# Attention in pairs of query tiles over four quarters of the array, with a softmax split over three engines and due times derived backwards

## Chip, cores, metric

One core of a Trainium2 chip. The metric is the device time of one launch in microseconds (us). The kernel before takes 608.16 us (median of 3 runs, 606.42 to 609.38). Five engines run their own queues in order: TensorE (PE; PEld is its weight load), VectorE (DVE), ScalarE (ACT), GpSimd (POOL) and SyncE (SP, which here issues the DMAs).

## What is computed

A windowed attention with block summaries, then two dense stages. The input has 2 batches, 8 heads, 768 positions and 64 dimensions, all fp32:

```python
k_sum = k.reshape(B, H, nb, 32, D).max(axis=3)
v_sum = v.reshape(B, H, nb, 32, D).mean(axis=3)
scores_l = where(|i - j| < 16, scale * q @ k.T, -1e9)
scores_s = scale * q @ k_sum.T + log(32)
a = softmax(concat([scores_l, scores_s]))
x = (a @ concat([v, v_sum])) as (1536, 512)
x = ((x @ w1) * (x @ w2)) @ w3 @ w_out      # widths 1024, 1024, 512
h = x @ w_in;  y = (h * clip(h + 3, 0, 6) / 6) @ w_out2
```

## The kernel before

Dense products run as three passes of fp32r matmuls: each operand is split into a high and a low part (`arena[:, s, 0]` and `[:, s, 1]`), and high x high, low x high and high x low are added. A weight chunk arrives as raw 64-bit data (512 KB into one of 4 `raw` buffers) and `convert` makes the two parts: ACT (L248, L254), DVE (L263, L267), ACT again (L271, high part), POOL (L275, low part). While the array has banks to spare (the W' part), the first steps of `convert` work in PSUM banks 4 and 5; later they work in the SBUF buffers `c`.

The parts of the program, in order of their data:

- **W'.** `wprime` multiplies w3 with w_out (transposed chunks, group 0 then group 1, 8 steps each, 12 matmuls a step, 24 chunks converted in all); `wprime_out` writes each group's 4 result banks as weights.
- **Attention.** `attend` works on one tile of 64 queries of all 8 heads. Per tile: `scores` (L405, 8 matmuls, one head in the upper 64 rows and columns of the array, the next in the lower, into bank 6), mask and maximum on DVE (L413, L418), 4 exponentials on ACT that also sum (L424), the inverse on DVE (L432, L433), the scaling on POOL (L438), 4 transposes on PE (L446, bank 7), a copy on ACT (L451), 8 matmuls with the values (L458, bank 7), and the split of the result into x's high part on ACT (L470) and low part on DVE (L474). 24 tiles; 8 make one block of 512 tokens. For the first block, keys are copied out of `kres` by DVE (L379); the summaries come from maxima on DVE (L310) and a chain of halving adds on POOL (L323).
- **First dense stage.** `ab(j, i)` multiplies block j of x with chunk i of w1 and w2 (24 matmuls into banks 4 and 5); `acc1` multiplies the product with W' into banks 0 to 3. `x2_out` writes the next x. Block 0's `ab` needs all 8 tiles of block 0 and the first converted w1 and w2 chunks. The tiles of later blocks are laid between the dense matmuls of the block before.
- **Second dense stage.** `hu`, `acc2` and `y_out`, 192 matmuls each of `hu` and `acc2` a block. With W' (192), `ab` (192 a block) and `acc1` (96 a block) that makes 2208 matmuls of 128 x 512 in all.

The order on each engine is not written by hand. Every operation is entered in a graph with its engine, an assumed duration and a **due time**; `Graph.schedule` simulates the engines and always starts the ready operation with the earliest due time. Before, due times come from a handful of constants (`DUE_W`, `DUE_Q`, `AHEAD`, `BEHIND` and others). A DVE or POOL operation marked `lock` waits in that simulation for the SBUF port that the two share.

Of the kernel before, what the change touches and what calls it, by code (L numbers as in the profile page):

```python
# [30 lines left out]
P = 128  # L31
# [9 lines left out]
NK = NWIN + NSUM  # L41
NPAIR = H // 2
# [4 lines left out]
TPK = TB // QT  # L47
# [10 lines left out]
class Graph:  # L58
# [6 lines left out]
    LAT = {"sp": 2100, "pe": 250}  # L65

# [21 lines left out]
    def schedule(self):  # L88
# [55 lines left out]
DUE_W = ((1.47, 2.38), (49.46, 3.51))  # L144
DUE_K, DUE_V, DUE_ROWS = 13.5, 5.9, 14.6
DUE_Q = (28.52, 6.4)
L3N = 1
DUE_FF = 90.7
AHEAD, BEHIND = 461.8, 280.8


def build(tc, qd, kw, vw, kt, vt, consts, wp_in, w12_in, w2_in, out):
# [13 lines left out]
    three = pool.tile([P, 32], F32, name="three")[:, 0:1]  # L166
# [47 lines left out]
    def load(due, out_fn, in_ap, nbytes, writes):  # L214
        g.op("sp", max(650, nbytes / 360.0), due, lambda: nc.sync.dma_start(out=out_fn(), in_=in_ap), (), writes)
# [98 lines left out]
    def sum32(due, x, c, key):  # L314
# [40 lines left out]
    def vsum_rows(due, b, bk):  # L355
        def fn():
            for p in range(NPAIR):
                nc.tensor.transpose(bank[bk][0:NK, p * P : (p + 1) * P], vsum[:, p, :], ident)

        g.op("pe", 460, due, fn, ["vsum", "con"], [("bank", bk)])  # L360

    def summary_cols(due, i, bk):
        g.op(
            "pool", 350, due, lambda: nc.gpsimd.tensor_copy(kall[i][:, :, NWIN:NK], ksum), ["ksum"], [("ks", i)]
        )
        g.op(
            "act", 600, due,
            lambda: nc.scalar.activation(
                out=vall[i][NWIN:NK, :], in_=bank[bk][NWIN:NK, :], func=AF.Copy, scale=1.0 / BLK
            ), [("bank", bk)], [("vs", i)],  # L370
        )

    def copy(eng, n, due, o, i, reads, writes):
        if eng == "act":
            g.op(eng, 190 + 0.86 * n, due, lambda: nc.scalar.activation(out=o, in_=i, func=AF.Copy), reads, writes)
        elif eng == "pool":
            g.op(eng, 60 + 3.5 * n, due, lambda: nc.gpsimd.tensor_copy(o, i), reads, writes)
        else:
            g.op(eng, 200 + 0.52 * n, due, lambda: nc.vector.tensor_copy(o, i), reads, writes, True)  # L379

    def attend(t, due, bs, bp, bx):

        i, i2 = t % 3, t % 2
        tt = t % TPB
        m = 0 if tt == 0 else 2 if tt == TPB - 1 else 1
        j, col = t // TPK, (t % TPK) * QT
        s0 = A_X + NPAIR * j
        ki, vi, si, pi, sti = kall[i], vall[i], sc[i2], pt[i2], st[i2]
        qs = qst[t // 2 % 2]
        if t % 2 == 0:  # L390
            load(due - 5 * us, lambda: qs, qd[t // 2], P * 2048, [("qs", t // 2 % 2)])
        if t < TPK:
            copy("dve", 410, due - 2 * us, ki[:, :, 0:NWIN], kres[:, :, t * QT : t * QT + NWIN],
                 [("kres", c) for c in range(3) if c * S // 3 + (WIN if c else 0) < t * QT + NWIN and t * QT < (c + 1) * S // 3 + WIN],
                 [("kw", i)])
        else:
            load(due - 5 * us, lambda: ki[:, :, 0:NWIN], kw[t], P * NWIN * 16, [("kw", i)])
        load(due - 4 * us, lambda: vi[0:NWIN, :], vw[t], NWIN * 2048, [("vw", i)])
# [11 lines left out]
        g.op("pe", 900, due, scores, [("kw", i), ("ks", i), ("qs", t // 2 % 2)], [("bank", bs)])  # L410

        def mask():
            nc.vector.scalar_tensor_tensor(  # L413
                out=si, in0=bank[bs][:, 0 : NPAIR * NK].rearrange("p (a n) -> p a n", a=NPAIR), scalar=SCALE,
                in1=con[:, m * NK : (m + 1) * NK].unsqueeze(1).to_broadcast((P, NPAIR, NK)),
                op0=ALU.mult, op1=ALU.add,
            )
            nc.vector.tensor_reduce(out=sti[:, 1, :], in_=si, op=ALU.max, axis=AX.X, negate=True)  # L418

        g.op("dve", 1340, due + 1 * us, mask, [("bank", bs), "con"], [("s", i2), ("st", i2)])  # L420

        def expo():
            for p in range(NPAIR):
                nc.scalar.activation(  # L424
                    out=si[:, p, :], in_=si[:, p, :], func=AF.Exp, bias=sti[:, 1, p : p + 1],
                    accum_out=sti[:, 2, p : p + 1],
                )

        g.op("act", 2300, due + 2.5 * us, expo, [], [("s", i2), ("st", i2)])

        def inv():
            nc.vector.tensor_scalar(out=sti[:, 0, :], in0=sti[:, 2, :], scalar1=1e-9, scalar2=None, op0=ALU.add)  # L432
            nc.vector.reciprocal(out=sti[:, 1, :], in_=sti[:, 0, :])  # L433
# [8 lines left out]
        g.op("pool", 1050, due + 4.2 * us, norm, [("st", i2)], [("s", i2)])

        def trans():
            for p in range(NPAIR):
                nc.tensor.transpose(bank[bp][0:NK, p * P : (p + 1) * P], si[:, p, :], ident)  # L446

# [336 lines left out]
```

## Time and profile before

| quantity | before |
|---|---|
| median of 3 runs | 608.16 us |
| profiled execution, own time | 606.42 us |
| its span | 604.6 us |
| PE busy | 573.9 us (95%) |
| DVE, ACT, POOL busy | 287.5, 294.3, 147.1 us |
| PE busy by tenths, first 8 slices of 15.1 us | 3 7 6 7 9 9 6 9, then 9 to the end |

A slice is a fortieth of the span. Busy time counts an instruction from its start to its modelled end, so a busy PE may still be slow; what matters is which engine the others wait for. An execution's own time is its span and a remainder, here 1.82 us.

### The profile page before, as it was taken

To read this page: it belongs to the slowest core of one execution; us is meant where nothing else is said; L and a number is where in the kernel's file an instruction comes from. 1 tells how busy PE (TensorE), PEld (TensorE's weight loads), DVE (VectorE), ACT (ScalarE), POOL (GpSimd) and SP (SyncE) were. 2 spreads that over 40 slices of the span, in tenths; PEclk is the share of its full clock that TensorE was granted. 3 is DMA by queue.
4 is the path that set the end of the run, shared out by engine and by line. 5 is a ranking of instruction groups with operands and counts; after the bars stand their busy time and mean duration, and the time that the engine had idled before them with its cause. 6 is when DMAs were issued, how large, how long until landed. Compare 5 with 4: busy or idle time off the path is not lost.

```text
span 604.6 us, 8171 instructions
## 1 busy us (share of the span) xinstructions
PE 573.9 (95%) x3080; PEld 460.6 (76%) x3080; DVE 287.5 (48%) x443; ACT 294.3 (49%) x645; POOL 147.1 (24%) x144
## 2 busy tenths in 40 slices
PE   3767996999999999999999999999999999999997
PEld 2556774777877777888888888888888888888886
DVE  4587759685774641837455862222222222222221
ACT  6868778774774645617555932222322222322222
POOL 4873434567431113303323430000000000000000
PEclk9897999999999999999999999999999999999999
DMA  8995557565665110532433200000100000100001
GB/s 291 329 292 194 161 169 213 166 203 169 233 214 144 41 28 1 161 118 69 142 140 124 86 0 1 0 1 0 70 1 1 0 1 0 71 0 1 0 1 69
DMA packets 29607, 59.04 MB, mean 98 GB/s; under 512 B 10624, under 2 KB 14080, under 8 KB 29568
## 3 DMA queue, kind: packets, MB, share of 16 engines
q1 hardware_dynamic: 29424, 58.39, 30.1%
q8 instruction: 24, 0.39, 0.3%
q14 instruction: 15, 0.12, 0.1%
q10 hardware_dynamic: 144, 0.13, 0.1%
HBM read 55.37 MB, written 3.15 MB: 97 GB/s over the span
## 4 chain that ended last, share of the span: by engine, by line
PE 89%; DMA 4%; DVE 3%; ACT 2%; issue 1%; POOL 0%; SPq 0%; DVEq 0%; POOLq 0%; ACTq 0%
PE bank L293 81%; DMA raw<-in_wp_dram 4%; PE bank L405 3%; PE bank L458 2%; PE bank L446 2%; ACT raw L254 1%; ACT bank L248 1%; DVE arena L608 1%; DVE c L267 1%; DVE sc L413 0%; DVE c L263 0%; DVE bank L263 0%; ACT arena L271 0%; DVE st L418 0%; DVE ksum L310 0%
## 5 line engine op out<-in xcount | busy, mean ns | idle before, releaser
L293 PE MATMUL bank<-arena 128*128 128x512 f32 x1344 | 334.2, 401 | 18.5 <-ACT arena L271 12.6
L293 PEld LDWEIGHTS bank<-arena 128*128 128x128 f32 x1344 | 253.1, 192 | 77.2 <-ACT arena L271 13.7
L543 ACT ACTIVATE ta<-bank,three 128x512 f32<-128x512 f32 x48 | 33.0, 688 | 149.3 <-PE bank L293 149.3
L293 PE MATMUL bank<-arena,w 128*128 128x512 f32 x432 | 105.4, 396 | 0.0
L547 DVE SCALAR_TENSOR_TENSOR tg<-ta,bank 128x512 f32<-128x512 f32 x48 | 33.0, 688 | 149.3 <-ACT ta L543 149.3
L293 PEld LDWEIGHTS bank<-arena,w 128*128 128x128 f32 x432 | 81.0, 188 | 19.0 <-issue 0.3
L275 POOL TENSOR_TENSOR arena<-c,arena 128x512 fp32r<-128x512 f32 (+1 forms) x50 | 65.2, 1311 | 76.2 <-ACT arena L271 71.4
L492 DVE TENSOR_TENSOR arena<-tg,arena 128x512 fp32r<-128x512 f32 x68 | 55.4, 815 | 37.1 <-ACT arena L487 36.7
L487 ACT ACTIVATE arena<-tg 128x512 fp32r<-128x512 f32 x72 | 45.4, 630 | 37.8 <-DVE tg L547 32.6
L254 ACT ACTIVATE raw<-raw 128x512 uint32<-128x512 uint32 (+1 forms) x74 | 47.7, 653 | 0.0
L438 POOL TENSOR_TENSOR sc<-sc,st 128x480 f32<-128x480 f32 x24 | 24.8, 1031 | 88.8 <-DVE st L433 66.5
L263 DVE SCALAR_TENSOR_TENSOR c<-c,raw 128x512 uint32<-128x512 uint32 x48 | 41.4, 870 | 10.2 <-ACT raw L254 10.0
L267 DVE SCALAR_TENSOR_TENSOR c<-raw,c 128x512 uint32<-128x512 uint32 x48 | 43.9, 931 | 0.5
L511 DVE TENSOR_TENSOR tg<-ta,bank 128x512 f32<-128x512 f32 x24 | 16.5, 687 | 52.8 <-PE bank L293 45.9
L424 ACT ACTIVATE sc<-sc,st 128x120 f32<-128x120 f32 x96 | 36.7, 386 | 8.3 <-DVE st L418 7.2
L248 ACT ACTIVATE c<-raw 128x512 f32<-128x512 f32 x48 | 31.3, 666 | 14.6 <-POOL w L275 5.2
L293 PE MATMUL bank<-w,arena 128*128 128x512 f32 x144 | 35.4, 394 | 0.0
L293 PE MATMUL bank<-late,arena 128*128 128x512 f32 x144 | 34.6, 389 | 0.0
L293 PE MATMUL bank<-arena,late 128*128 128x512 f32 x144 | 34.4, 389 | 0.0
L509 ACT ACTIVATE ta<-bank 128x512 f32<-128x512 f32 x24 | 14.3, 596 | 38.2 <-PE bank L293 38.2
L271 ACT ACTIVATE arena<-c 128x512 fp32r<-128x512 f32 (+1 forms) x50 | 29.9, 607 | 6.0 <-DVE c L267 4.2
L293 PEld LDWEIGHTS bank<-w,arena 128*128 128x128 f32 x144 | 27.0, 188 | 6.4
(48 smaller groups left out, 419.7 us busy)
## 6 DMA issues: line engine op xcount, KB each, us to landing
raw<-in_w_dram SPq DMA_DIRECT2D x48, 512.0 KB, 3.9
raw<-in_wp_dram SPq DMA_DIRECT2D x22, 512.0 KB, 5.5
vall<-in_vw_dram SPq DMA_DIRECT2D x24, 192.0 KB, 2.6
qst<-in_q_dram SPq DMA_DIRECT2D x12, 256.0 KB, 2.8
kall<-in_kw_dram SPq DMA_DIRECT2D x16, 192.0 KB, 3.2
out_dram<-c SPq DMA_DIRECT2D x11, 256.0 KB, 2.0
vres<-in_vt_dram SPq DMA_DIRECT2D x3, 512.0 KB, 6.6
raw<-in_kt_dram SPq DMA_DIRECT2D x3, 512.0 KB, 4.4
```

The costliest lines, as they stand in the source:

```text
L248: lambda uf=uf, wf=wf: nc.scalar.activation(out=uf, in_=wf[:, :, 1], func=AF.Copy, scale=2.0**-112),
L254: lambda lw=lw: nc.scalar.activation(out=lw, in_=lw, func=AF.Copy, scale=2.0**-29 * (1 - eps), bias=7.5 * eps - 0.5),
L263: lambda ui=ui, lw=lw: nc.vector.scalar_tensor_tensor(out=ui, in0=ui, scalar=3, in1=lw, op0=ALU.logical_shift_left, op1=ALU.bitwise_or),
L267: lambda ci=ci, ui=ui, hw=hw: nc.vector.scalar_tensor_tensor(out=ci, in0=hw, scalar=0x80000000, in1=ui, op0=ALU.bitwise_and, op1=ALU.bitwi ...
L271: lambda cf=cf, e=e: nc.scalar.activation(out=slot(s)[:, 0, e], in_=cf, func=AF.Copy),
L275: lambda cf=cf, e=e, eng=eng: eng.tensor_tensor(out=slot(s)[:, 1, e], in0=cf, in1=slot(s)[:, 0, e].bitcast(F32), op=ALU.subtract),
L293: nc.tensor.matmul(out=out_ap, lhsT=lhs(a), rhs=rhs(c), start=start and n == 0, stop=stop and n == 3 * len(terms) - 1,)
L424: nc.scalar.activation(out=si[:, p, :], in_=si[:, p, :], func=AF.Exp, bias=sti[:, 1, p : p + 1], accum_out=sti[:, 2, p : p + 1],)
L487: g.op("act", 630, due, lambda: nc.scalar.activation(out=slot(s)[:, 0, :], in_=src_ap, func=AF.Copy), [src_key], [("t", s, 0)])
L492: lambda: eng.tensor_tensor(out=slot(s)[:, 1, :], in0=src_ap, in1=slot(s)[:, 0, :].bitcast(F32), op=ALU.subtract), [src_key, ("t", s, 0)], ...
L543: g.op("act", 600, due, lambda: nc.scalar.activation(out=t, in_=bank[b], func=AF.Relu, bias=three), [("bank", b), "three"], [("ta", n % 2)])
L547: lambda: nc.vector.scalar_tensor_tensor(out=u, in0=t, scalar=6.0, in1=bank[b], op0=ALU.min, op1=ALU.mult), [("bank", b), ("ta", n % 2)], ...
```

## The change

- Attention works on **pairs** of tiles (12 pairs). `probabilities(u)` holds all up to the probabilities, `attend(u)` the rest. The scores of a pair are 16 matmuls, in groups of four that lie in four different 64 x 64 quarters of the array; the even tile's go to one bank and the odd tile's to another (banks 6 and 7). The keys of a pair are one stretch of 160 with the summaries on both sides, so the even tile has its summaries first and the odd tile last.
- The softmax of a pair is: two masks (DVE, L428), one maximum over 960 columns (DVE, L442), a subtraction (POOL, L444), one exponential (ACT, L445), one sum and the inverse (DVE, L448 to L450), a multiplication (POOL, L454). The transposed probabilities are copied by ACT for the even tile and by DVE for the odd one (L471, L469). The split of x is 512 columns wide.
- Summary rows of the values come from 8 plain matmuls instead of 4 transposes, at two partition offsets.
- **Due times.** Only PE's operations keep one; every other operation's is derived backwards from its users. All constants are new. `later_tiles` lays the pairs of later blocks every second `ab`.

```diff
     LAT = {"sp": 2100, "pe": 250}
+    LAST = 1e9
...
+        due = [o[2] if o[0] == "pe" else self.LAST for o in self.ops]
+        for i in range(n - 1, -1, -1):
+            for u in users[i]:
+                e = self.ops[i][0]
+                due[i] = min(due[i], due[u] - self.ops[i][1] - self.LAT.get(e, 40))
...
-DUE_W = ((1.47, 2.38), (49.46, 3.51))
+DUE_W = ((21.66, 11.07), (25.01, 4.7))
...
+            for lo, v in ((0, vsum[:, :, 32:]), (64, vsum)):
+                for p in range(NPAIR):
+                    nc.tensor.matmul(
+                        out=bank[bk][lo : lo + v.shape[2], p * P : (p + 1) * P], lhsT=v[:, p, :], rhs=ident,
+                        start=True, stop=True,
+                    )
...
             for p in range(NPAIR):
-                for h in range(2):
-                    pr = slice(h * D, (h + 1) * D)
-                    nc.tensor.matmul(
-                        out=bank[bs][pr, p * NK : (p + 1) * NK], lhsT=qs[pr, t % 2, p, :], rhs=ki[pr, p, :],
-                        start=True, stop=True,
-                    )
...
+                for x in range(2):
+                    for h in range(2):
+                        pr, o = slice(h * D, (h + 1) * D), (h + x) % 2 * D
+                        lo = x * (KS - NK)
+                        nc.tensor.matmul(
+                            out=bank[bk[x]][o : o + D, p * NK : (p + 1) * NK], lhsT=qs[pr, x, p, :],
+                            rhs=ki[pr, p, lo : lo + NK], start=True, stop=True,
+                        )
...
-        def expo():
-            for p in range(NPAIR):
-                nc.scalar.activation(
-                    out=si[:, p, :], in_=si[:, p, :], func=AF.Exp, bias=sti[:, 1, p : p + 1],
-                    accum_out=sti[:, 2, p : p + 1],
-                )
...
+        g.op("pool", 2000, due + 3 * us,
+             lambda: nc.gpsimd.tensor_tensor(out=s8, in0=s8, in1=wide(0), op=ALU.subtract), [("st", i2)], skeys)
+        g.op("act", 1020, due + 4 * us, lambda: nc.scalar.activation(out=s1, in_=s1, func=AF.Exp), [], skeys)
...
+        g.op("pool", 2000, due + 5.5 * us,
+             lambda: nc.gpsimd.tensor_tensor(out=s8, in0=s8, in1=wide(1), op=ALU.mult), [("st", i2)], skeys)
...
+                fn = lambda: nc.vector.tensor_copy(pt[1][0:NK, :], bank[bk[1]][0:NK, :])
...
-        for t in range(TPK):
-            attend(t, (DUE_Q[0] + DUE_Q[1] * t) * us, 6, 7, 7)
+        for u in range(PPK):
+            at = (DUE_Q[0] + DUE_Q[1] * u) * us
+            probabilities(u, at, (6, 7))
+            if u:
+                attend(u - 1, at - DUE_Q[1] * us, 6, 7)
```

In the rows that follow, bank_75 to bank_78 are the result banks 0 to 3, bank_79 and bank_80 are banks 4 and 5, bank_81 and bank_82 are banks 6 and 7. On PE, before, around the first `ab` (bank_79, x12), which is where the attention of block 0 has to be complete:

```order
L293 MATMUL bank_78<-arena 128x512 x3
L405 MATMUL bank_81<-kall_91,qst_97 64x120 x8
L446 MATMUL bank_82<-con,sc_100 120x128 x4
L458 MATMUL bank_82<-pt_102,vall_95 64x64 x8
L405 MATMUL bank_81<-kall_92,qst_98 64x120 x8
L446 MATMUL bank_82<-con,sc_99 120x128 x4
L293 MATMUL bank_79<-arena 128x512 x12
```

The same place after the change:

```order
L479 MATMUL bank_81<-pt_102,vall_96 64x64 x2
L302 MATMUL bank_76<-arena 128x512 x3
L302 MATMUL bank_77<-arena 128x512 x3
L302 MATMUL bank_78<-arena 128x512 x3
L302 MATMUL bank_75<-arena 128x512 x3
L302 MATMUL bank_76<-arena 128x512 x3
L302 MATMUL bank_79<-arena 128x512 x12
L302 MATMUL bank_80<-arena 128x512 x12
L302 MATMUL bank_79<-arena 128x512 x12
L302 MATMUL bank_80<-arena 128x512 x12
L302 MATMUL bank_77<-arena 128x512 x3
```

Before, all 192 matmuls of W' and the scores of 11 tiles stand ahead of the first `ab`. Now the last matmuls of W' (group 1) stand on both sides of it: 162 of them ahead, 30 behind, and ahead of it the scores of 5 pairs and the rest of 4.

On DVE, before, the piece with the first two tiles' softmax:

```order
L413 SCALAR_TENSOR_TENSOR sc_99<-bank_81,con 128x480
L418 TENSOR_REDUCE st_103<-sc_99 128x4
L263 SCALAR_TENSOR_TENSOR bank_79<-bank_79,raw_62 128x512
L379 COPY kall_91<-kres 128x4x96
L608 TENSOR_TENSOR arena<-bank_75,arena 128x512
L608 TENSOR_TENSOR arena<-bank_76,arena 128x512
L608 TENSOR_TENSOR arena<-bank_77,arena 128x512
L608 TENSOR_TENSOR arena<-bank_78,arena 128x512
L413 SCALAR_TENSOR_TENSOR sc_100<-bank_81,con 128x480
L418 TENSOR_REDUCE st_104<-sc_100 128x4
```

And after:

```order
L428 SCALAR_TENSOR_TENSOR sc_99<-bank_81,con 128x480
L428 SCALAR_TENSOR_TENSOR sc_99<-bank_82,con 128x480
L272 SCALAR_TENSOR_TENSOR bank_79<-bank_79,raw_64 128x512
L442 TENSOR_REDUCE st_103<-sc_99 128x8
L272 SCALAR_TENSOR_TENSOR bank_80<-bank_80,raw_65 128x512
L276 SCALAR_TENSOR_TENSOR c_68<-raw_64,bank_79 128x512
L276 SCALAR_TENSOR_TENSOR c_69<-raw_65,bank_80 128x512
L402 COPY kall_91<-kres 128x4x160
L428 SCALAR_TENSOR_TENSOR sc_100<-bank_81,con 128x480
```

The first softmax has moved ahead of the output of W' group 0 (L608, now L630) and stands between the conversions of its chunks. On SP, the first loads before:

```order
L215 DMA raw_62<-in_wp_dram 128x256 x2
L215 DMA raw_63<-in_wp_dram 128x256 x2
L215 DMA raw_64<-in_wp_dram 128x512
L215 DMA raw_65<-in_wp_dram 128x512
L215 DMA con<-in_con_dram 128x488
L215 DMA vres<-in_vt_dram 128x1024
L215 DMA raw_62<-in_wp_dram 128x512
```

And after:

```order
L224 DMA raw_62<-in_wp_dram 128x256
L224 DMA raw_63<-in_wp_dram 128x256
L224 DMA vres<-in_vt_dram 128x1024
L224 DMA raw_62<-in_wp_dram 128x256
L224 DMA raw_63<-in_wp_dram 128x256
L224 DMA vres<-in_vt_dram 128x1024 x2
L224 DMA raw_64<-in_wp_dram 128x512
L224 DMA raw_65<-in_wp_dram 128x512
L224 DMA kres<-in_kt_dram 128x4x272
```

The keys and values for the summaries (`kres`, `vres`) now go ahead of the chunks of W' step 1 and later.

## Rows read from the trace of the kernel before

**Rows 1.** The page: busy time by engine, then the last-ended chain's shares.

```profile
PE 573.9 (95%) x3080; PEld 460.6 (76%) x3080; DVE 287.5 (48%) x443; ACT 294.3 (49%) x645; POOL 147.1 (24%) x144
...
PE 89%; DMA 4%; DVE 3%; ACT 2%; issue 1%; POOL 0%; SPq 0%; DVEq 0%; POOLq 0%; ACTq 0%
```

**Rows 2.** The chain that ended last, in order: start, us, what.

```profile
36.60 9.50 DMA raw<-in_wp_dram
...
95.95 1.97 DVE c L263 x2
...
235.76 365.37 PE bank L293 x1596
601.16 0.39 ACT c L569
```

**Rows 3.** Busy us of each engine by stretch; then clock, DMA share, GB/s.

```profile
0.00:46.00 46.00, 27.53 (x106) 19.56 (x107) 28.48 (x44) 31.25 (x58) 30.71 (x42) 0.96 0.93 305
46.00:60.00 14.00, 10.80 (x86) 8.46 (x86) 10.41 (x24) 12.19 (x38) 4.57 (x5) 0.78 0.58 186
60.00:92.00 32.00, 31.71 (x269) 24.56 (x268) 20.91 (x40) 24.51 (x69) 12.57 (x11) 1.00 0.56 169
92.00:103.47 11.47, 6.16 (x79) 4.47 (x77) 10.39 (x21) 10.40 (x35) 4.21 (x4) 1.00 0.70 185
0.00:103.47 103.47, 76.21 (x537) 57.06 (x537) 70.19 (x127) 78.35 (x198) 52.05 (x61) 0.95 0.74 234
103.47:601.20 497.73, 497.65 (x2547) 403.53 (x2544) 216.84 (x316) 215.61 (x447) 95.07 (x84) 1.00 0.21 69
```

**Rows 4.** The same chain, one by one, around 110 us.

```profile
108.06 0.61 PE bank L458 x16
108.67 0.97 PE bank L405 x16
109.64 2.95 PE bank L293 x12
112.59 0.44 PE bank L446 x4
113.03 2.77 PE bank L293 x12
```

**Rows 5.** Groups of PE from 103.47 us: count, busy, mean ns.

```profile
L405 PE MATMUL bank<-kall,qst 64*64 64x120 f32 x208 | 13.5, 269 | 0.0
L458 PE MATMUL bank<-pt,vall 120*64 120x64 f32 x256 | 11.0, 228 | 0.0
L446 PE MATMUL bank<-con,sc 128*120 128x128 f32 x63 | 9.6, 275 | 0.0
```

**Rows 6.** PE in order of time: start, us, operation.

```profile
42.19 1.04 PE L405 MATMUL bank<-kall,qst 64*64 64x120 f32 x16
...
103.47 4.59 PE L293 MATMUL bank<-arena 128*128 128x512 f32 x12
```

**Rows 7.** DMA up to 46 us: the total, and a weight chunk.

```profile
DMA packets 5657, 14.04 MB, mean 305 GB/s; under 512 B 503, under 2 KB 2167, under 8 KB 5654
...
raw<-in_wp_dram SPq DMA_DIRECT2D x18, 512.0 KB, 5.6
```

**Rows 8.** Groups by form over the whole span: count, busy us, mean ns.

```profile
L267 DVE SCALAR_TENSOR_TENSOR c<-raw,c 128x512 uint32<-128x512 uint32 x48 | 43.9, 931 | 0.5
L263 DVE SCALAR_TENSOR_TENSOR c<-c,raw 128x512 uint32<-128x512 uint32 x48 | 41.4, 870 | 10.2 <-ACT raw L254 10.0
...
L438 POOL TENSOR_TENSOR sc<-sc,st 128x480 f32<-128x480 f32 x24 | 24.8, 1031 | 88.8 <-DVE st L433 66.5 <-ACT pt L451 9.5 <-ACT sc L424 8.5
...
L413 DVE SCALAR_TENSOR_TENSOR sc<-bank,con 128x480 f32<-128x480 f32 x24 | 15.7, 655 | 19.0 <-PE bank L446 9.6 <-PE bank L405 9.2
...
L263 DVE SCALAR_TENSOR_TENSOR bank<-bank,raw 128x512 uint32<-128x512 uint32 x22 | 15.3, 697 | 9.9 <-ACT raw L254 9.5
...
L267 DVE SCALAR_TENSOR_TENSOR c<-raw,bank 128x512 uint32<-128x512 uint32 x22 | 14.9, 683 | 1.1
...
L470 ACT ACTIVATE arena<-bank 128x256 fp32r<-128x256 f32 x24 | 9.1, 379 | 13.5 <-PE bank L458 13.5
...
L608 DVE TENSOR_TENSOR arena<-bank,arena 128x512 fp32r<-128x512 f32 x8 | 5.2, 684 | 1.6 <-ACT arena L604 1.5
...
L604 ACT ACTIVATE arena<-bank 128x512 fp32r<-128x512 f32 x8 | 4.4, 597 | 0.8 <-PE bank L293 0.6
...
L433 DVE RECIPROCAL st<-st 128x4 f32<-128x4 f32 x24 | 4.3, 178 | 0.8
...
L310 DVE TENSOR_REDUCE ksum<-kres 128x32 f32<-128x1024 f32 x3 | 3.7, 1218 | 1.9 <-DMA kres<-in_kt_dram 1.9
```

**Rows 9.** DVE in order of time: the last step of the first tile.

```profile
57.39 0.42 DVE L474 TENSOR_TENSOR arena<-bank,arena 128x256 fp32r<-128x256 f32 x1 [0.54 <-ACT arena L470]
```

More of the change, by code (lines that the diff above doesn't have):

```diff
@@ L373, in copy @@
[L373 to L377, printed above, removed]
-        else:
[L379 to L398, printed above, removed]
@@ new lines, in summary_v, with probabilities @@
+            lambda: nc.scalar.activation(out=vall[i][rows, :], in_=bank[bk][rows, :], func=AF.Copy, scale=1.0 / BLK),
+            [("bank", bk)], [("vs", i)],
+        )
+    def probabilities(u, due, bk):
+        i2, uu = u % 2, u % PPB
+        ki, si, sti, qs = kall[i2], sc[i2], st[i2], qst[i2]
+        vi = [2 * i2, 2 * i2 + 1]
+        load(due - 5 * us, lambda: qs, qd[u], P * 2048, [("qs", i2)])
+        if u < PPK:
+            lo = u * 2 * QT
+            g.op("dve", 600, due - 2 * us,
+                 lambda: nc.vector.tensor_copy(ki[:, :, NSUM : NSUM + KW], kres[:, :, lo : lo + KW]),
+                 [("kres", c) for c in range(3) if c * S // 3 + (WIN if c else 0) < lo + KW and lo < (c + 1) * S // 3 + WIN],
+                 [("kw", i2)], True)
+        else:
+            load(due - 5 * us, lambda: ki[:, :, NSUM : NSUM + KW], kw[u], P * KW * 16, [("kw", i2)])
+        for h in range(2):
+            rows = slice(0, NWIN) if h else slice(NSUM, NK)
+            load(due - 4 * us, lambda h=h, rows=rows: vall[vi[h]][rows, :], vw[2 * u + h], NWIN * 2048, [("vw", vi[h])])
@@ new lines, in probabilities @@
+        g.op("pe", 1100, due, scores, [("kw", i2), ("ks", i2, 0), ("ks", i2, KS - NSUM), ("qs", i2)],
+             [("bank", b) for b in bk])
+        for x in range(2):
+            m = (0 if uu == 0 else 1) if x == 0 else (3 if uu == PPB - 1 else 2)
+            g.op(
+                "dve", 660, due + 1 * us,
+                lambda x=x, m=m: nc.vector.scalar_tensor_tensor(
+                    out=si[:, x], in0=bank[bk[x]][:, 0 : NPAIR * NK].rearrange("p (a n) -> p a n", a=NPAIR),
+                    scalar=SCALE, in1=con[:, m * NK : (m + 1) * NK].unsqueeze(1).to_broadcast((P, NPAIR, NK)),
+                    op0=ALU.mult, op1=ALU.add,
+                ), [("bank", bk[x]), "con"], [("s", i2, x)],
+            )
@@ L442, in attend @@
[L442 to L453 removed]
+        g.op("dve", 1560, due + 5 * us, inv, skeys, [("st", i2)])
@@ L455, in pv @@
         def pv():
             for p in range(NPAIR):
-                for h in range(2):
-                    nc.tensor.matmul(
-                        out=bank[bx][h * D : (h + 1) * D, p * QT : (p + 1) * QT],
-                        lhsT=vi[0:NK, (2 * p + h) * D : (2 * p + h + 1) * D],
-                        rhs=pi[0:NK, p * P + h * QT : p * P + (h + 1) * QT], start=True, stop=True,
-                    )
-        g.op("pe", 600, due + 6.6 * us, pv, [("pt", i2), ("vw", i), ("vs", i)], [("bank", bx)])
@@ L465, in attend @@
-        xb = bank[bx][:, 0 : NPAIR * QT].rearrange("p (a n) -> p a n", a=NPAIR)
-        xh = ar[:, s0 : s0 + NPAIR, 0, col : col + QT]
-        xl = ar[:, s0 : s0 + NPAIR, 1, col : col + QT]
+                for x in range(2):
+                    for h in range(2):
+                        o = p * P + (h + x) % 2 * D
+                        nc.tensor.matmul(
+                            out=bank[b0][h * D : (h + 1) * D, p * P + x * QT : p * P + (x + 1) * QT],
+                            lhsT=vall[vi[x]][0:NK, (2 * p + h) * D : (2 * p + h + 1) * D],
+                            rhs=pt[x][0:NK, o : o + QT], start=True, stop=True,
+                        )
@@ L634, in build, with later_tiles @@
                 later_sums(T1 + 5 * 3 * GRP)
+        def later_tiles(u, at):
+            if PPB <= u < PPB + 2:
+                vsum_rows(at, 7)
+                summary_k(at, u % 2)
+                for r in range(2):
+                    summary_v(at, 2 * (u % 2) + r, 7)
+            if u < NTILE // 2:
+                probabilities(u, at, (6, 7))
+            attend(u - 1, at - 2 * 3 * GRP, 6, 7)
+        later_tiles(PPK, T1 - 3 * GRP - AHEAD * us)
         due = T1
```

152 lines of the change are left out of this document (78 added, 74 removed).

## The prediction

> **What bounds the kernel now.** I read the page first: PE is busy for 95% of the span, the others for half or less, and the chain that ended last runs through PE for 89% [rows 1]. So the time is PE's work plus what PE waits. The chain in order of time says where it waits: up to about 46 us it goes through DMA (a wait of 9.50 us from 36.60 on), around 100 us through DVE, and from 235.76 us it is one piece of 1596 matmuls to the last result at 601.16 us [rows 2]. The busy time by stretch shows the same: from 103.47 us to the end PE is busy for 497.65 of 497.73 us, and ahead of that it is not full; up to 46 us the DMA is at 0.93, from 92 to 103.47 us DVE is busy for 10.39 of 11.47 us [rows 3]. At 103.47 us the first `ab` starts. I therefore cut the time in three: T, the start of the first `ab`; D, the dense stretch behind it; and the rest, 604.60 - 601.20 = 3.40 us at the end of the span and 606.42 - 604.60 = 1.82 us outside it, 5.2 us that nothing here touches. Before: 103.47 + 497.73 + 5.2 = 606.4.
>
> **D, the dense stretch.** One matmul of 128 x 512 takes 365.37 / 1596 = 0.229 us of PE's chain [rows 2].
>
> - *W' moved behind.* 30 of its 192 matmuls now stand behind the first `ab`: +30 x 0.229 = +6.9 us. They leave T's part, where PE waits anyway.
> - *Scores.* A tile's 8 matmuls are 16 records and take 0.97 us, 61 ns a record; 4 transposes of 128 columns are 4 records in 0.44 us, 110 ns each; 8 value matmuls of 64 columns are 16 records in 0.61 us, 38 ns each [rows 4]. If the records ran one after the other at the transposes' rate, 120 columns would take 103 ns and 64 columns 55 ns. So two halves of the array overlap already: half of 103 is 51.5, and 9 ns a record come on top; half of 55 is 27.5, and 10.5 come on top. The trace of before shows no four quarters at once. Bounds: no more overlap than now, 2 x 0.97 = 1.94 us a pair; full overlap of four with nothing on top, 32 x 103 / 4 = 0.82 us. I take four with the same 10 ns, 32 x 36 ns = 1.15 us, since the extra looks alike at two sizes. In this stretch stand the scores of 13 tiles (208 records), and 16 tiles each of transposes and values (63 and 256 records) [rows 5]; now scores of 7 pairs: 13 x 0.97 = 12.6 becomes 7 x 1.15 = 8.1, -4.5 us. Transposes and value matmuls stay in number and size: 0.
> - *After scores,* 12 matmuls take 2.95 us against 2.77 us elsewhere [rows 4], 0.2 us for the change of shape; 6 fewer such changes: -1.2 us.
> - *Value summaries:* 8 plain matmuls of 128 columns. Bounds: 8 x 110 ns, and two records each, 16 x 110 ns; 1.3 us between them, twice in this stretch, in place of one set of 0.44 us: +2.2 us.
> - *Cold start.* The first 12 `ab` matmuls took 4.59 us [rows 6], behind a wait of PE; elsewhere 2.77. If PE comes from W' matmuls, as the new order has it: -1.8 us.
>
> D = 497.7 + 6.9 - 4.5 - 1.2 + 2.2 - 1.8 = 499.3 us. Attention's PE work ahead of T is hidden under waits, and earns nothing by itself.
>
> A rule weighed against the rows: the Trainium skill, "TensorEngine Tiling (Array Packing)", Gotcha 1 under Restrictions and Gotchas, says that different row tiles cannot access the same PSUM bank simultaneously. Here the two heads of one tile are different row tiles of one bank. By that sentence nothing would overlap beyond the two banks. The rows disagree already for before, where both heads go to bank 6 and take 61 ns where one at a time would take 103.
>
> **T, the start of the first ab.** It needs x of block 0 (4 pairs now) and the first two weight chunks of `ab`.
>
> *Up to the last chunk of W' group 0.* Before, 14.04 MB had moved by 46 us, at 305 GB/s [rows 7]. The new queue has ahead of and with that last chunk: 16 weight chunks of 0.524 MB, `vres` 1.57, `kres` 1.64, `con` 0.31, 4 q of 0.26, 4 v of 0.20, together 13.8 MB. So it lands at about 46 us; this part stays DMA's, and the softmax of the first pairs lies under it. Moving `vres` and `kres` ahead costs PE idle time early, but what it waits for later is the same sum of bytes.
>
> *From there to T.* Now DVE is nearly full. Its order has 48 instructions from the conversion of that chunk to the last x of block 0, priced from [rows 8]: 20 conversion steps in banks, 0.69 each, 13.8; 4 in `c`, 0.87 and 0.93, 3.6; 6 masks of 0.655, 3.9; 2 maxima and 2 sums over 960 columns at 1.218 x 960 / 1024 = 1.14, 4.6; 4 small ones of 0.18, 0.7; 10 of 512 columns out of banks (copy of the probabilities, x's low part, W' low part) at 0.684, 6.8. Sum 33.4 us. Between 46 and 60 us before, DVE's share was 74%, in its full stretch 91% [rows 3]. I take the middle, 83%: 40 us, and 2 us for the copy of the last weight parts: T = 46 + 40 + 2 = 88 us.
>
> The other engines allow this. ACT loses per pair: before 2 x (1.6 + 0.6 + 0.38), the exponentials with their sums 1.6; now one exponential of about 0.60 + 448 x 0.85 ns = 0.98, where 0.85 ns is (597 - 379) / 256 per column, and two of 0.597 [rows 8]: 5.2 becomes 2.2. POOL gains: 2 x 2 x 1.031 instead of 2 x 1.031, +2.1 us a pair. POOL was busy for 52 us up to 103.47 [rows 3]; with 4 pairs done it has some 62 us of work ahead of T, which it starts at about 7 us.
>
> Bounds of T: below, the bytes. The queue up to the second weight chunk of `ab` is 21.3 MB, 70 us at 305 GB/s, and about 7 us for the conversion of two chunks: 77 us. Above: at the share of 62% that DVE had up to 46 us [rows 3], 46 + 54 + 2 = 102 us.
>
> **Sum.** 88 + 499.3 + 5.2 = 592.5 us against 606.4 of the same execution, -14 us: -15.5 from T, +1.5 from D. That profiled execution is the fastest of three, 1.7 us under the median of 608.16; I put the median of after at 593.
>
> **Rivals.**
>
> - *A. The quarters do not overlap beyond two.* 7 pairs x (1.94 - 1.15) = 5.5 us: 598. For it: all four share input rows or output columns with two others, and no row shows that combination. Against: the 10 ns a record look like issue, not like a conflict.
> - *B. Only the bytes pace T.* T = 77: 582. For it: instructions of DVE overlap a little in the trace, so the sum of means overstates. Against: DVE, ACT and POOL would all have to be over 85% busy for 70 us.
> - *C. The pair's chain is the bound, and the kernel becomes slower.* A pair's steps on its own are scores 1.15, masks 1.31, maximum 1.14, subtraction 2.06, exponential 0.98, sum and inverse 1.5, multiplication 2.06, transposes 0.88, copies 0.68, values 1.22, x's parts 1.28: 14.3 us in a row, twice through POOL, each step behind conversions on a queue in order. The first tile before took from 42.19 us to 57.39 + 0.42 [rows 6, 9], 15.6 us for about 7.7 us of own work, a factor of 2. So a pair may take 28 us. Scores, transposes and values of neighbours share banks 6 and 7. The first scores need the last `kres` chunk, 6.7 MB into the queue, about 22 us, and 5 us more: 27 us. With two pairs in flight, the four end at 27 + 2 x 28 = 83 us and T holds. With one in flight they end at 27 + 4 x 28 = 139 us, and the time is 139 + 499.3 + 5.2 = 643.5. It decides from 18 us a pair on, where T reaches 99 and the gain is gone; from 20 us it is slower than before.
> - *D. Block 0's dense part stalls on DVE.* From T to the second pair of block 1, DVE has about 37 us of work under 46 us of PE. Where both inputs lie in SBUF the conversion steps cost 0.87 and 0.93 us against 0.70 and 0.68 us with one in a bank [rows 8]; POOL is now busier beside them. If all DVE work under POOL became a third dearer, 37 would become 49 and some 3 us a stretch would show, three stretches: 9 us, 601. The Trainium skill, "GPSIMD Engine Reference", Specifications, says that POOL's SBUF interfaces contend with DVE instructions that have two SBUF inputs; the trace agrees, by those two pairs of numbers.
>
> **How the numbers follow.** Forecast (T from 82 to 97, quarters overlap) 0.55; A 0.12; B 0.12; C 0.15; D 0.06. The likeliest gives 593. The range leaves out most of C and the lowest end of B: 580 to 607. A change within 0.5%, 605.1 to 611.2 against the median, can't be told from none. All but C lie below: faster 0.84; C is split, 0.08 same and 0.08 slower.
>
> **What would show it.** Right: the first `ab` at 82 to 97 us and PE full behind it; 0.97 to 1.3 us in the chain for a pair's scores; DVE over 80% busy from 46 us to T, with PE waiting for x's low part. Wrong: PE waiting for POOL's multiplication of the probabilities with DVE half idle (C); a pair's scores near 1.9 us (A); gaps of PE in front of `acc1` behind T (D).

## The result, and the profile after

| | before | after |
|---|---|---|
| median | 607.42 us (606.42 to 609.38, 4 runs) | 587.04 us (586.08 to 590.71, 4 runs) |
| profiled execution: own time, span | 606.42, 604.6 us | 586.08, 584.3 us |
| T, start of the first `ab` | 103.47 us | 84.75 us |
| D, from there to the end of the last matmul | 497.73 us | 495.82 us |
| PE busy | 573.9 us | 555.4 us |

The ratio of after to before is 0.967, 95% interval 0.962 to 0.972. The forecast was 593 us, from 580 to 607. One execution of experiment 3 below, of 826.36 us at a granted clock of 0.661, is left out as disturbed.

The page of after: busy time by engine, and the shares of the last-ended chain.

```profile
PE 555.4 (95%) x3120; PEld 451.9 (77%) x3120; DVE 303.4 (52%) x415; ACT 262.3 (45%) x443; POOL 167.8 (29%) x146
...
PE 90%; DVE 4%; POOL 2%; issue 1%; ACT 1%; DMA 1%; SPq 0%; DVEq 0%
```

The chain of after in order of time (start, us, what). Here and, unless said otherwise, in the kernels that follow, L302 are the 128 x 512 matmuls, L417 the scores, L464 the transposes, L479 the value matmuls, L370 the value summaries:

```profile
10.11 5.57 POOL vres L332 x9
17.26 3.83 PE bank L370 x16
...
65.26 1.03 PE bank L479 x28
66.29 7.02 PE bank L302 x30
73.32 0.98 PE bank L417 x32
...
76.60 0.87 PE bank L464 x8
77.47 2.76 PE bank L302 x12
80.24 1.08 PE bank L479 x32
81.32 40.34 PE bank L302 x177
...
138.73 2.01 PE bank L370 x16
...
169.34 1.22 DVE sc L428 x2
...
175.96 29.78 PE bank L302 x130
...
223.78 2.99 PE bank L302 x12
...
252.82 327.68 PE bank L302 x1443
```

The value matmuls that end at 81.32 us are those of block 0's last pair. In PE's order 15 matmuls of W' follow, 15 x 0.229 = 3.4 us, and then the first `ab`: T = 84.75 us. The last matmul ends at 580.50 us (252.82 + 327.68); D is counted to 580.57 us, as it was to 601.20 us before, where the last matmul ended at 601.13. A pair's scores take 0.98 us; a set of value summaries takes 2.01 us, and 3.83 the first time.

The busy time of after by stretch (length; PE, PEld, DVE, ACT, POOL; clock, DMA share, GB/s), where [rows 3] show before:

```profile
0.00:46.00 46.00, 24.38 (x174) 18.02 (x175) 33.12 (x48) 29.18 (x53) 27.94 (x40) 0.96 0.85 297
46.00:65.26 19.26, 15.95 (x161) 12.05 (x159) 18.35 (x31) 17.23 (x33) 16.13 (x12) 1.00 0.84 270
65.26:84.75 19.49, 19.49 (x166) 15.90 (x167) 16.43 (x27) 15.22 (x28) 12.83 (x10) 1.00 0.81 268
0.00:84.75 84.75, 59.82 (x498) 45.97 (x499) 67.89 (x104) 61.63 (x110) 56.90 (x61) 0.98 0.84 284
84.75:580.57 495.82, 495.57 (x2623) 405.90 (x2621) 235.07 (x311) 200.36 (x334) 110.91 (x86) 1.00 0.21 68
```

PE is full from 65.26 us on, and its idle time of 84.75 - 59.82 = 24.9 us lies ahead of that. The waits of PE in after (by what, us in total, times, longest):

```profile
PE bank L302 <- ACT arena L280: 12.5, 3, 9.3
PE bank L370 <- POOL vsum L332: 6.3, 1, 6.3
PE bank L302 <- POOL arena L284: 1.7, 2, 0.9
PE bank L479 <- ACT pt L471: 1.7, 2, 0.9
PE bank L417 <- DVE arena L496: 1.7, 1, 1.7
```

Most of it is the start: 9.3 us until the first chunk is converted and 6.3 us until POOL has the value sums. The waits inside the pairs' chains are small, and POOL's multiplication of the probabilities is not among them.

One thing in the trace has nothing to do with the order of the work. PE's groups by form after 176 us (count, busy us, mean ns of one), of after:

```profile
L302 PE MATMUL bank<-arena,w 128*128 128x512 f32 x336 | 80.1, 391 | 0.0
L302 PE MATMUL bank<-w,arena 128*128 128x512 f32 x144 | 34.6, 389 | 0.0
L302 PE MATMUL bank<-late,arena 128*128 128x512 f32 x144 | 34.6, 389 | 0.0
```

And of before:

```profile
L293 PE MATMUL bank<-arena,w 128*128 128x512 f32 x354 | 86.2, 395 | 0.0
L293 PE MATMUL bank<-w,arena 128*128 128x512 f32 x144 | 35.4, 394 | 0.0
L293 PE MATMUL bank<-late,arena 128*128 128x512 f32 x144 | 34.6, 389 | 0.0
```

`w` and `late` are weight tiles of one shape in two pools. Before, the matmuls that read a tile of `w` took 4 to 5 ns longer each than after, where they take nearly what the others take.

### The profile page after: what moved, and what is told of

Its sections match the earlier page's. It is cut to its first block, busy times and chain, and to the rows that moved or that the text cites. A ratio compares the mean times of both kernels' runs of the same rounds, so it can differ in the third digit from the quotient of the medians.

```text
span 584.3 us, 7946 instructions
## 1 busy us (share of the span) xinstructions
PE 555.4 (95%) x3120; PEld 451.9 (77%) x3120; DVE 303.4 (52%) x415; ACT 262.3 (45%) x443; POOL 167.8 (29%) x146
## 4 chain that ended last, share of the span: by engine, by line
PE 90%; DVE 4%; POOL 2%; issue 1%; ACT 1%; DMA 1%; SPq 0%; DVEq 0%
PE bank L302 83%; PE bank L479 2%; PE bank L417 2%; PE bank L464 1%; PE bank L370 1%; POOL vres L332 1%; DVE c L276 1%; POOL arena L284 1%; DMA raw<-in_wp_dram 1%; DVE bank L272 1%; DVE st L448 1%; DVE sc L428 0%; DVE st L442 0%; DVE pt L469 0%; ACT raw L263 0%
## 5 line engine op out<-in xcount | busy, mean ns | idle before, releaser
L302 PE MATMUL bank<-arena 128*128 128x512 f32 x1344 | 322.9, 395 | 14.4 <-ACT arena L280 12.5
L302 PEld LDWEIGHTS bank<-arena 128*128 128x128 f32 x1344 | 250.9, 189 | 70.6 <-ACT arena L280 13.0
L302 PE MATMUL bank<-arena,w 128*128 128x512 f32 x432 | 103.4, 391 | 0.0
L302 PEld LDWEIGHTS bank<-arena,w 128*128 128x128 f32 x432 | 80.6, 188 | 17.1 <-issue 0.3
L514 DVE TENSOR_TENSOR arena<-tg,arena 128x512 fp32r<-128x512 f32 x68 | 52.5, 772 | 36.5 <-ACT arena L509 36.3
L272 DVE SCALAR_TENSOR_TENSOR c<-c,raw 128x512 uint32<-128x512 uint32 x48 | 47.1, 997 | 5.1 <-ACT raw L263 5.1
L263 ACT ACTIVATE raw<-raw 128x512 uint32<-128x512 uint32 (+1 forms) x74 | 47.2, 654 | 0.0
L444 POOL TENSOR_TENSOR sc<-sc,st 128x960 f32<-128x960 f32 x12 | 22.2, 1854 | 51.5 <-DVE st L442 51.5
L302 PE MATMUL bank<-w,arena 128*128 128x512 f32 x144 | 34.6, 389 | 0.0
L302 PE MATMUL bank<-late,arena 128*128 128x512 f32 x144 | 34.6, 389 | 0.0
L302 PE MATMUL bank<-arena,late 128*128 128x512 f32 x144 | 34.4, 389 | 0.0
L302 PEld LDWEIGHTS bank<-arena,late 128*128 128x128 f32 x144 | 27.0, 188 | 5.6
L302 PEld LDWEIGHTS bank<-late,arena 128*128 128x128 f32 x144 | 27.0, 188 | 5.6
```

The source lines that it names most:

```text
L263: lambda lw=lw: nc.scalar.activation(out=lw, in_=lw, func=AF.Copy, scale=2.0**-29 * (1 - eps), bias=7.5 * eps - 0.5),
L272: lambda ui=ui, lw=lw: nc.vector.scalar_tensor_tensor(out=ui, in0=ui, scalar=3, in1=lw, op0=ALU.logical_shift_left, op1=ALU.bitwise_or),
L302: nc.tensor.matmul(out=out_ap, lhsT=lhs(a), rhs=rhs(c), start=start and n == 0, stop=stop and n == 3 * len(terms) - 1,)
L444: lambda: nc.gpsimd.tensor_tensor(out=s8, in0=s8, in1=wide(0), op=ALU.subtract), [("st", i2)], skeys)
L514: lambda: eng.tensor_tensor(out=slot(s)[:, 1, :], in0=src_ap, in1=slot(s)[:, 0, :].bitcast(F32), op=ALU.subtract), [src_key, ("t", s, 0)], ...
```

## The experiments

The forecast's theory: four quarters overlap (D), and DVE sets T. All kernels with pairs stand beside 587.04 us of after; the runs of before in the same sessions had medians of 607.6 to 608.1 us.

**1. Two quarters in place of four.** Against after, the odd tile's heads go to the same two quarters as the even tile's:

```diff
-                        pr, o = slice(h * D, (h + 1) * D), (h + x) % 2 * D
+                        pr, o = slice(h * D, (h + 1) * D), h * D
...
-                        o = p * P + (h + x) % 2 * D
+                        o = p * P + h * D
```

> The odd tile's heads go to the same two quarters as the even tile's; order on every engine, instruction counts and sizes stay. If four quarters at once are what brought a pair's scores from 1.94 to 0.98 us, a pair takes about 1.9 us again: 7 pairs behind the first ab and one or two in the full stretch ahead of it make 7 to 9 us, about 595. If the records are bound by their issue and not by the quarters (32 records in 0.98 us are 31 ns each), nothing changes: 587.

594.98 us (594.40 to 596.47), ratio 0.978 (0.976 to 0.981). The scores in its chain:

```profile
75.28 1.79 PE bank L417 x32
```

The quarters overlap, and rival A falls: 1.79 us with two, 0.98 with four, for the same 32 records. Behind T this is 7 x 0.81 = 5.7 us; T itself is 87.49 us, 2.7 us later.

**2. Pairs without the new due times.** Against after, the due times are taken as entered, with the constants of before (a pair every 12.8 us where a tile had 6.4):

```diff
-        due = [o[2] if o[0] == "pe" else self.LAST for o in self.ops]
...
+        due = [o[2] for o in self.ops]
-DUE_W = ((21.66, 11.07), (25.01, 4.7))
-DUE_K, DUE_V, DUE_ROWS = 106.6, -119.0, -31.9
-DUE_Q = (118.14, 0)
+DUE_W = ((1.47, 2.38), (49.46, 3.51))
+DUE_K, DUE_V, DUE_ROWS = 13.5, 5.9, 14.6
+DUE_Q = (28.52, 12.8)
 L3N = 1
-DUE_FF = 6.5
-AHEAD, BEHIND = -26.4, -143.7
+DUE_FF = 90.7
+AHEAD, BEHIND = 461.8, 280.8
```

> Pairs as in the changed kernel, but every operation's due time and all constants as in the kernel before (a pair every 12.8 us in place of a tile every 6.4). The first ab then stands behind all 192 matmuls of W'. If the due times made T (84.8 us) short, T goes back to about 100 and the time to about 600, since 30 matmuls or 6.9 us move from the dense stretch to T's part. If the lighter attention made it, T is at 90 (the 6.9 us of W' and little else) and the time stays within 1% of 587.

605.18 us (604.01 to 607.29), ratio 0.996 (0.994 to 0.999). Its chain around the first `ab` (L298; L413 the scores), which starts at 100.58 us:

```profile
98.70 1.88 PE bank L413 x32
100.58 4.74 PE bank L298 x12
...
113.20 3.35 DMA raw<-in_w_dram
...
120.01 5.06 PE bank L298 x21
```

All W' matmuls stand ahead of T again; the first `ab` starts slowly (4.74 us for 12, at a granted clock of 0.60 from 100.58 to 105.30 us, between its two levels of 1.2 and 2.4 GHz; before, 4.59 in [rows 6]), and a weight chunk for the next one comes late.

**3. The new due times without pairs.** Against before, the derivation and all new constants, with single tiles:

```diff
+        due = [o[2] if o[0] == "pe" else self.LAST for o in self.ops]
+        for i in range(n - 1, -1, -1):
...
-DUE_FF = 90.7
-AHEAD, BEHIND = 461.8, 280.8
+DUE_FF = 6.5
+AHEAD, BEHIND = -26.4, -143.7
```

> Attention in single tiles as before, with due times derived backwards and the new constants. If the due times made T short, T is about 90 us and the time about 606.4 - 13.5 + 6.9 = 600 (162 matmuls ahead of the first ab). If the lighter attention made it, T stays near 100 and the time is 606 to 612.

613.04 us (612.14 to 613.17), ratio 1.007 (1.005 to 1.010). The same kernel, run again for its trace:

> The same kernel as the one with single tiles and due times derived backwards, which took 613 us, for a trace at the full clock. If the single tiles' heavier ACT work (5.2 us in place of 2.2 for two tiles) is late under the new order, ACT is over 90% busy ahead of the first ab and T is above 103 us. If instead the dense stretch is at fault, T is below 100 us and PE waits behind it.

612.08 us (610.57 to 612.75), ratio 1.006 (1.003 to 1.009). PE becomes dense at 91.89 us and T is 94.1 us, but PE does not stay dense behind T. Two stretches:

```profile
170.00:210.00 40.00, 37.05 (x268) 29.81 (x267) 17.45 (x34) 17.83 (x54) 3.95 (x4) 1.00 0.36 105
250.00:350.00 100.00, 97.11 (x515) 78.64 (x512) 66.78 (x87) 66.20 (x134) 37.88 (x27) 0.97 0.34 110
```

PE idles 2.95 and 2.89 us there, with DVE and ACT far from full. T comes 9.4 us earlier than before, and D is 513.4 us, 15.7 longer, of which 30 matmuls of W' explain 6.9: what the early start gains is given back behind it.

**4. Pairs and the derivation, with the constants of before.** The edit is that of experiment 2 without its lines on `due`, so the derivation stays.

> Pairs, due times derived backwards from PE's, but PE's own due times by the old constants, so PE's order is near that with forward due times (186 matmuls of W' ahead of the first ab). If the derivation is what brings loads and conversions in time, the late w1 and w2 chunks behind the first ab are gone and the time is 588 to 594. If the order on PE does it, T stays at 95 to 100 and the time at 598 to 605.

600.34 us (599.41 to 601.79), ratio 0.987 (0.984 to 0.989). So of the 18 us between experiment 2 and after, the derivation, put in first, brings 5, and the constants, which set PE's own order, then 13. In this kernel all 192 W' matmuls stand ahead of the first `ab` (not 186, as the expectation has it), against 162 in after. T is 98.9 us and D 495.2: the 13 us of the constants lie in T.

**5. The exponentials on ACT.** Eight exponentials with bias and sum, in place of POOL's subtraction, one exponential and DVE's sum:

```diff
-             lambda: nc.gpsimd.tensor_tensor(out=s8, in0=s8, in1=wide(0), op=ALU.subtract), [("st", i2)], skeys)
...
+                nc.scalar.activation(
+                    out=s8[:, k, :], in_=s8[:, k, :], func=AF.Exp, bias=sti[:, 0, k : k + 1],
+                    accum_out=sti[:, 2, k : k + 1],
+                )
```

> The softmax as before: 8 exponentials of 120 columns a pair on ACT with bias and sum, no subtraction on POOL, no sum over 960 columns on DVE. ACT gets 2.2 us more a pair, POOL 1.9 and DVE 1.1 less. If T is bound by DVE (busy 18.4 of 19.3 us from 46 to 65 us), T falls by 2 to 4 us: 583 to 585. If the relief of ACT is what counted, T grows by 3 us or more: 590 or more.

590.34 us (589.97 to 592.71), ratio 0.970 (0.968 to 0.972): its interval meets that of after, so any gain of the split over three engines is at most small. With its other durations the planner also made another order (159 W' matmuls ahead of the first `ab`, T 89.5 us in a trace of 592.71), so this is not the split alone.

**6. Both copies of the probabilities on ACT.**

> Both copies of the transposed probabilities on ACT: DVE 0.68 us less a pair, ACT 0.60 more. If DVE paces the part up to 65 us (18.4 of 19.3 us busy from 46 us on), T falls by 1 to 2 us: 585 to 586. If the bytes or the chain of steps pace it, 587; if ACT becomes late, 588 to 590.

589.28 us (586.09 to 590.51), ratio 0.967 (0.963 to 0.971): no difference from after that stands clear of the scatter. Here, too, the order is another (165 W' matmuls ahead of the first `ab`).

**7. Value summaries by 4 transposes.** POOL's last adds write the sums to both places of a wider `vsum`, and one set of transposes moves them; to make room, `three` shrinks from 64 to 8 floats.

```diff
-    three = pool.tile([P, 64], F32, name="three")[:, 0:1]
+    three = pool.tile([P, 8], F32, name="three")[:, 0:1]
...
-            for lo, v in ((0, vsum[:, :, 32:]), (64, vsum)):
...
+                nc.tensor.transpose(bank[bk][0:NK, p * P : (p + 1) * P], vsum[:, p, :], ident)
```

> The value summaries by 4 transposes again, with POOL writing the sums at both offsets (3 more adds of 32 columns per batch). In the changed kernel the 8 plain matmuls take 2.01 us twice behind the first ab, 4 transposes 0.44: -3.1 us, and up to 3 us ahead of it, where the first set took 3.8 us at the lower clock with ACT waiting: 581 to 584. If the place ahead is paced by the bytes, only the 3.1 us: 584. If the new order that the planner makes of it costs as much, 587.

594.43 us (592.04 to 594.92), ratio 0.976 (0.974 to 0.979), slower than after. The planner, which sees other durations, made another order, and at the boundary to block 1 the chain of this kernel is one of DVE (L425 masks, L272 conversion):

```profile
163.97 1.88 DVE arena L511
...
168.54 1.79 DVE arena L548 x3
170.33 1.13 DVE sc L425 x2
...
173.72 2.80 DVE c L272 x2
...
177.16 4.84 PE bank L302 x13
```

From 150 to 180 us PE is busy for 25.36 us only, and DVE for 29.02 (29.83 and 23.61 in after). This is what rival D described. The expectation puts the first set's 3.8 us down to a lower clock; the trace of after has a granted clock of 1.00 from 17.26 to 21.09 us, so why that set takes nearly twice as long stays open.

**8. The same exchange in the order of after.** The extra adds stand inside the old operations, and the planner's durations stay, so every engine keeps its order.

> The kernel after in its own order on every engine, with one exchange: the last adds of the value summaries write the sums to both places on POOL, and 4 transposes of 120 columns put them into the bank in place of 8 plain matmuls. Theory (the prediction's term for the value summaries was too small: 2.01 us a set measured where 1.3 was put, and a plain fp32 matmul costs more than a transpose): a set takes 0.45 us as the transposes of the probabilities do, twice in the dense stretch, so 2 x 1.56 = 3.1 us less there; ahead of the first ab nothing, since PE waits there anyway: 584 us. Rival (the extra adds of POOL come late, or the new order of e5 was not the cause of its stall at the boundary to block 1): 587 or above, with a wait of PE near 170 us.

589.44 us (588.02 to 589.73), ratio 0.969 (0.967 to 0.971): a miss. Its chain (L368 the summaries):

```profile
68.00 8.63 PE bank L302 x30
...
84.61 40.40 PE bank L302 x177
...
142.32 0.44 PE bank L368 x4
...
154.25 0.58 PE bank L368 x4
...
253.50 330.65 PE bank L302 x1443
```

The transposes gave most of what was expected: from T (84.61 + 3.43 = 88.04 us) to the last piece it takes 165.46 us, after takes 168.07, so 2.6 us less, where 3.1 were expected; and PE waits at the boundary for 0.2 us, as in after. But the last piece, the same 1443 matmuls in the same order, takes 330.65 us where after takes 327.68: +2.97. By form:

```profile
L302 PE MATMUL bank<-arena,w 128*128 128x512 f32 x336 | 82.1, 396 | 0.0
L302 PE MATMUL bank<-w,arena 128*128 128x512 f32 x144 | 35.6, 395 | 0.0
```

It is the difference of before, back again: the smaller `three` has moved `w`. By the starts in the two traces, 2.5 of the 2.97 us lie in the 384 matmuls of this piece that read `w`.

And T came 3.3 us later. 1.7 us of it are there when a piece of 30 matmuls starts (68.00 us, 66.29 in after), and 1.6 are these 30, 8.63 us for 7.02. The granted clock was 0.83 from 67 to 77 us, between the two levels, where after has 1.00. It was 0.83 from 50 to 60 us, too, behind a wait of PE of 2.35 us (1.69 in after). But PE's waits just ahead of 67 us are no longer than in after (0.74 and 0.71 us against 0.91 and 0.72), so what lowered the clock there is open, and so is whether the edit did it.

**9. DVE's reductions halved.** In the order of after, the maximum and the sum go over 60 of 120 columns (`in_=s8[:, :, 30:90]`).

> The kernel after in its own order, with the maximum and the sum over 60 of the 120 columns of each row (the middle ones); so the softmax is not complete, and only its time is meant. Each of the two reductions falls from 1.14 to about 0.6 us. Theory (DVE sets the start of the first ab, as the prediction has it): 4 pairs x 2 x 0.54 = 4.3 us less on DVE ahead of it, so T falls from 84.75 to 81 or so and the time to 583. Rival (PE's own work and the bytes set it, DVE has room): T within 1 us of 84.75, 586 to 588.

586.90 us (586.01 to 588.75), ratio 0.966 (0.962 to 0.969): no gain. In its trace the chain up to 57 us has left DVE:

```profile
33.60 7.95 DMA raw<-in_wp_dram
...
45.44 5.06 DMA raw<-in_wp_dram
...
83.43 40.34 PE bank L302 x177
```

DVE's wait for the parts of chunks (its L272 for ACT's L263) grows from 12.2 us to 17.3 up to T. T is 86.86 us in this execution. 1.5 us of this delay do not come from the edit: PE's first matmuls start that much later, before there are any scores. In after, then here:

```profile
9.34 1.65 PE L302 MATMUL bank<-arena 128*128 128x512 f32 x3 [9.34 <-ACT arena L280]
```

```profile
10.87 1.65 PE L302 MATMUL bank<-arena 128*128 128x512 f32 x3 [10.87 <-ACT arena L280]
```

If those 1.5 us carry through, T would be about 85.4 us without them, still not the 81 that DVE as the bound asked for.

**10. POOL's two steps halved,** the subtraction and the multiplication over the first 60 columns.

> The kernel after in its own order, with the subtraction and the multiplication on POOL over 60 of the 120 columns of each row; so the probabilities are not right, and only the time is meant. Each falls from 1.85 to about 1.0 us. Theory (DVE and PE set the start of the first ab; POOL's steps lie under them): 587, T within 1 us of 84.75. Rival (the chain of a pair, twice through POOL, is what PE waits for ahead of the first ab): 8 x 0.85 = 6.8 us less in four chains, two in flight, so some 3.4 us off T: 583 to 584.

589.23 us (585.87 to 590.02), ratio 0.968 (0.965 to 0.972): the same as after within the scatter, and T is 81.55 + 3.43 = 84.98 us. The pair's way through POOL costs nothing that shows here.

**11. 1.05 MB more on the DMA queue,** into `ta` and `tg`, which are idle until T:

```diff
-            load(dv, lambda c=c: vres[:, c], vt[0, c], P * 4096, [("vres", c)])
...
+                for k, x in enumerate((ta, tg)[c] if c < 2 else ()):
+                    x = x.rearrange("p (a n) -> p a n", a=2)
+                    nc.sync.dma_start(out=x, in_=vt[0, c, :, 2 * k : 2 * k + 2])
+                nc.sync.dma_start(out=vres[:, c], in_=vt[0, c])
```

> The kernel after in its own order, with 1.05 MB of additional loads on SP's queue, ahead of the first two chunks of the values for the summaries, into buffers that nothing uses before the first ab. Theory (up to 46 us bytes are the limit, as the prediction has it, but not the only one up to the first ab): 1.05 MB at 297 GB/s is 3.5 us; the last chunk of W' group 0 lands that much later and most of it goes into T: 589.5 to 590.5. Rival (only DVE, or PE's own work, sets T): 587 to 588.

589.59 us (588.73 to 590.54), ratio 0.970 (0.968 to 0.972). The medians alone don't separate it from after. Its trace (L376 the summaries; PE's first matmuls, then the chain):

```profile
10.86 1.65 PE L302 MATMUL bank<-arena 128*128 128x512 f32 x3 [10.86 <-ACT arena L280]
```

```profile
5.30 7.05 DMA vres<-in_vt_dram
...
19.66 3.81 PE bank L376 x16
...
84.76 40.36 PE bank L302 x177
```

The sums come 2.4 us later than in after, and T (84.76 + 3.43 = 88.19 us) is 3.4 us later, about the 3.5 us of the added bytes. But PE's first matmuls are 1.5 us late here as they were in experiment 9, which adds no bytes; against that execution T is only 1.3 us later. That more bytes move T is likely, and not shown.

## Why the prediction was right, and where its steps were off

The profiled execution has 586.08 = 84.75 + 495.82 + 5.51 us, against 592.5 = 88 + 499.3 + 5.2 forecast. Of the 6.4 us, 3.3 are T and 3.5 are D; the rest is 0.3 longer.

**D.** Term by term, measured against forecast: the scores gave 12.6 - 7 x 0.98 = 5.7 us, not 4.5. Twelve matmuls after a change of shape still take 2.99 against 2.76 us, so -1.2 stands. The cold start is gone: the first `ab` lies in a piece of 177 matmuls at 0.228 us each; -1.8 stands. The value summaries are the term that was mis-sized: 2.01 us a set, 126 ns a record, and not 1.3; two sets for one of 0.44 are +3.6, not +2.2. That value lies above the upper bound that was set (16 x 110 ns = 1.76 us): the transposes' rate was taken as a plain matmul's. Two terms that the forecast put at nothing were small and partly cancel: the value matmuls take 1.08 us a pair where two tiles took 2 x 0.61 [rows 4], -1.1 us for 8 pairs, and one tile's 4 transposes (0.44 us) that stood just ahead of T in the old order stand behind it now, +0.4. With W' (+6.9) this makes 497.7 + 6.9 - 5.7 - 1.2 + 3.6 - 1.8 - 1.1 + 0.4 = 498.8 us. **The step that failed is one that the sum did not have:** the place of `w`. 432 + 144 matmuls read it. Before, they took 5 to 6 ns more than those on `late`; 576 x 6 ns = 3.5 us, and 495.3 us are left, with 495.8 measured. Experiment 8 shows this price in one piece: 2.97 us in 1443 matmuls, of which 384 read `w`. The change itself has the line, `three` from 32 to 64 floats, and the two means were in the trace of before.

**T.** The bounds held, and 88 was close, but its reason, DVE as the engine that sets T, was not borne out, so the closeness is in part luck. DVE was busy for 34.78 of the 38.75 us from 46 us to T, 90%, as the list of signs wanted it. The other half of that sign failed: ahead of T, PE waits for x's low part (L496) once, 1.7 us up to 49.31 us, and then it is full for 19.5 us up to T. And with 4 pairs x 2 reductions halved, some 4 us off DVE's queue, nothing was gained (experiment 9): DVE then waits for chunks. POOL's steps do not move T either (10). More bytes probably do (11), so rival B's mechanism may have been in play together with DVE; yet T is not the 77 us of B. How T divides between bytes, DVE and PE's own work stays open: three kernels with one order differ by 2 us in T (84.75 in after, 84.98 and 86.86 in experiments 10 and 9, which have less to do), and 1.5 of the 2 us are there at PE's first matmuls.

**The rivals.** A fell (experiment 1). C fell: PE does not wait for L454 (POOL's multiplication), and T does not move with POOL's steps. D did not happen in this order but is close: at 175.96 us the chain comes through DVE, and PE waits 0.2 us; another order of nearly the same work (experiment 7) falls into it. The price that D is built on is in the trace of before: of the 96 conversion steps with both inputs in SBUF, the 61 beside an idle POOL took 0.68 us on average, the 28 with POOL busy for over half of their time 1.40.

**The two halves of the change work together.** Pairs alone: 605.2 us, and this kernel has the fast `w`; due times alone: 612 to 613, with the slow one, as before. Neither gains by itself beyond that placement; together they take 20.4 us off, of which the placement is about 3.5. Pairs with the derivation, but PE's order by the old constants, take 600.3 (experiment 4). What the trace shows of it: with the old order, T stays behind all of W' (100.58 us in experiment 2, 103.47 before), so PE time saved by pairs ahead of T only lengthens its waits; with the new order and single tiles, the stretch behind T stalls (experiment 3). That pairs are what prevents these stalls was not shown step by step, and single tiles had the constants of the pairs: whether others would let them gain was not tried.

## What to carry to other kernels

Cut the time where PE becomes full: ahead of it only what arrives last counts, and an engine at 90% need not be it, so relieve it once on the chip before calling it the bound. Look at the start of both traces before reading a shift of a microsecond or two as the effect of an edit: here 1.5 us of one stood ahead of everything that was edited. Compare mean durations of one instruction on different tiles before and after an edit, and read changes of buffer sizes in a diff as changes of place: here one small tile was worth 3 us. An improvement that changes a planner's input is to be measured twice, with the new order and with the old order held.

## What was unexpected in the hardware

- **The place of a weight tile.** The program places `w` at byte 161,152 of each partition in after and in experiment 2, at 161,024 in before and experiment 3, and at 160,928 in experiments 7 and 8. The matmuls on it took 389 to 391 ns on average in the first case and 394 to 397 in the others. The two pools of the other operands start at 1,152 (`arena`) and 196,480 (`late`). By 256 bytes, these two and the fast place leave a remainder of 128, the slow places 0 and 160. That it is this remainder which counts is a guess; no run changed it alone.
- **Four quarters.** 32 records of 64 x 64 x 120 take 0.98 us, 31 ns each; in two quarters 1.79 us, 56 ns. The Trainium skill, "TensorEngine Tiling (Array Packing)", Gotcha 1 under Restrictions and Gotchas, has different row tiles unable to access one PSUM bank simultaneously. The trace does not agree: two row tiles write to each of two banks here, and two records at a time would take 32 x 103 ns / 2 = 1.65 us, an estimate from the prediction's 103 ns a record.
- **A plain fp32 matmul of 128 columns** costs 2.01 us for 8 (16 records of 126 ns), a transpose of as many 0.44 us for 4 (4 records of 110 ns): the plain one runs as two records.
